# A fused attention and MLP kernel: the row-sum product moves into the MLP's PSUM ring, which goes from two banks to three

## The chip, the cores and the metric

The kernel runs on one core of a Trainium2 chip. The metric is the device time of one execution in microseconds (us); shorter is better. The engines are called as the profile calls them: PE (TensorE, matmul), PEld (its weight loads), DVE (VectorE), ACT (ScalarE), POOL (GpSimd) and SP (which issues transfers).

## The reference, cut to what matters

```python
# attention: 8 batches, 12 heads, 448 positions, head size 64
scores = q @ k.T / 8
e = exp(scores - max)                               # softmax with one more term in the sum
attn = e / (sum(e) + exp(-max) + 1e-9)
x = (attn @ v)  -> 3584 tokens x 768
# MLP: 768 -> 2048 -> 768
h = x @ w_in;  g = relu(h)**2;  out = g @ w_out
```

## The kernel before

The kernel works through 48 pairs of heads ("units"; those of the first batch are cut in two). While a unit's scores, exponentials and values run, TensorE fills its time with matmuls of the MLP of tokens that are already done: generators hand them out in shares (`drain`), between the steps of attention. The MLP's first product works on blocks of 128, 256, 512 or 384 tokens; each of its PSUM tiles ("mp") takes 6 matmuls per 128 features and is then read by a relu and squared.

```python
s_psum  = tile_pool(name="s_psum",  bufs=2, space=PSUM)     # scores: 2 tiles of 2 banks
xz_psum = tile_pool(name="xz_psum", bufs=1, space=PSUM)     # xp and zp: one bank each
m_psum  = tile_pool(name="m_psum",  bufs=2, space=PSUM)     # "mp": 2 banks
...
def row_sums(u, es):                    # sums over the keys, by a product with ones
    zp = xz_psum.tile([128, 512], FP32, name="zp")
    for h in range(2):
        nc.tensor.matmul(zp[64*h:64*h+64, 0:n], ones, of_head(total, u, h), start=True, stop=True)
    nc.scalar.activation(out=lnz, in_=zp, func=AF.Ln, bias=one_b)       # last reader of zp
    nc.scalar.activation(out=rcp, in_=lnz, func=AF.Exp, scale=-1.0)
...
def mlp_in(t0, n):                      # first product of the MLP
    for f0 in range(0, NFFB, per):
        hp = m_psum.tile([128, 512], FP32, name="mp")
        ...                             # matmuls; a yield after each
        if t0 == 0: nc.scalar.activation(out=rt, in_=hp, func=AF.Relu)
        else:       nc.vector.tensor_scalar(out=rt, in0=hp, scalar1=0.0, op0=ALU.max)
        nc.vector.tensor_mul(g, rt, rt)
...
# one unit, in program order
xp = xz_psum.tile([128, 512], FP32, name="xp")
scores(u, et, 0);  drain(share * 0.45);  scores(u, et, 1)
rcp = row_sums(prev, pes);  values(prev, pet, xp, 0);  values(prev, pet, xp, 1)
drain(share * 0.15)
for step in range(3):
    add_chunks(u, et, es, step)         # VectorE sums the exponentials: "es"
    drain(share * (0.15, 0.1, 0.15)[step])
normalise(prev, xp, rcp)                # VectorE: xt = xp * rcp
```

Transposes of the first two batches and idle "warm" matmuls of the start take their tiles from `m_psum` too.

The softmax here doesn't subtract the row's maximum and nothing guards it: scores larger than these inputs give would overflow.

Of the kernel before, what the change touches and what calls it, by code (L numbers as in the profile page):

```python
# [8 lines left out]
FP32 = mybir.dt.float32  # L9
# [6 lines left out]
def kernel(  # L16
# [37 lines left out]
    osb_pool = ctx.enter_context(tc.tile_pool(name="osb", bufs=2))  # L54

    s_psum = ctx.enter_context(tc.tile_pool(name="s_psum", bufs=2, space=bass.MemoryType.PSUM))
    xz_psum = ctx.enter_context(tc.tile_pool(name="xz_psum", bufs=1, space=bass.MemoryType.PSUM))
    m_psum = ctx.enter_context(tc.tile_pool(name="m_psum", bufs=2, space=bass.MemoryType.PSUM))

    ctx.enter_context(tc.manual_schedule())  # L60
    nc.scalar.preload_act_table_set("natural_log_exp_and_others")
# [13 lines left out]
    def load_v(b, p0, p1):  # L75
        hs = slice(2 * p0, 2 * p1)
        if b not in vns:
            vns[b] = v_pool.tile([P, H, RUN, D], FP16, name="vn")
        nc.gpsimd.dma_start(out=vns[b][:, hs], in_=v_r[b, :, hs])  # L79
# [29 lines left out]
    def stage(b):  # L109
        for n, t in (("q", q), ("k", k)):  # L110
            st = nc.dram_tensor(f"stage_{n}{b}", (TOTAL,), FP16, kind="Internal").ap()
            stages[n, b] = st
            src = t.rearrange("b h s d -> (b h s d)")
            lo = b * HSD - FRONT
            hi = min(lo + TOTAL, B * HSD)
            m = (hi - lo) // 1024 * 1024
            for x, y in ((lo, lo + m), (lo + m, hi)):
                if y > x:
                    w = min(y - x, 1024)
                    nc.gpsimd.dma_start(out=st[x - lo:y - lo].rearrange("(r w) -> r w", w=w),  # L120
                                        in_=src[x:y].rearrange("(r w) -> r w", w=w))
            if hi < lo + TOTAL:
                nc.gpsimd.dma_start(out=st[hi - lo:TOTAL].rearrange("(r w) -> r w", r=1),
                                    in_=src[0:lo + TOTAL - hi].rearrange("(r w) -> r w", r=1))
# [11 lines left out]
    def regroup(b, pr):  # L136
        for name in "qk":
            f = flat.tile([P, RUN, 2, D], FP16, name=f"flat{name}")
            nc.vector.tensor_copy(f, naturals[name, b, pr].rearrange("p h t d -> p t h d"))
            flats[name, b, pr] = f  # L140

    def transposes(b, pr):
        tp = m_psum.tile([128, 2, 512], FP16, name="mp")
        for i, name in enumerate("qk"):
            for s in range(RUN):
                nc.tensor.transpose(tp[:, i, P * s:P * s + P], flats[name, b, pr][:, s], ident[0:P, 0:P])  # L146
        if b not in qks:
            qks[b] = qk_pool.tile([128, 3, COLS], FP16, name="qk")
        nc.vector.tensor_copy(qks[b][:, 0:2, pr * S:(pr + 1) * S], tp[:, :, 0:S])
# [13 lines left out]
    def scores(u, et, c):  # L163
        b, pr, q0, n = u
        qk = qks[b]
        two = [] if n == S else s_psum.tile([P, 2, 512], FP32, name="sp")
        for kk in (2 * c, 2 * c + 1):
            sp = s_psum.tile([P, 2, 512], FP32, name="sp") if n == S else two
            if b in ON_PE:
                o = 0 if n == S else kk % 2 * n  # L170
                for h in range(2):
                    r = slice(64 * h, 64 * h + 64)
                    x = pr * S
                    nc.tensor.matmul(sp[:, h, o:o + n], qk[r, 1, x + P * kk:x + P * kk + P],  # L174
                                     qk[r, 0, x + q0:x + q0 + n], start=True, stop=True)
            else:
                for h in range(2):
                    for odd in range(2):
                        r = slice(64 * odd, 64 * odd + 64)
                        x = (2 * pr + h) * (S // 2)  # L180
                        kx = x + kk // 2
                        which = 1
                        if kk % 2 != odd:
                            which = 2
                            kx += kk % 2
                        nc.tensor.matmul(sp[:, odd, h * (S // 2):(h + 1) * (S // 2)],  # L186
                                         qk[r, which, kx:kx + 2 * P - 1:2], qk[r, 0, x:x + S // 2],
                                         start=True, stop=True)
            if n == S:
                exp(chunk(et, u, c, kk).rearrange("p (o x) -> p o x", o=2), sp[:, :, 0:S])  # L190
        if n < S:
            exp(et[:, 0:RUN * 2 * n].rearrange("p (c h x) -> p c h x", c=2, h=2)[:, c], two[:, :, 0:2 * n])
# [16 lines left out]
    def of_head(e, u, h):  # L209

        b, _, _, n = u
        if n < S:
            return e[:, h]
        if b in ON_PE:
            return e.rearrange("p (h x) -> p h x", h=2)[:, h]
        return e.rearrange("p (o h x) -> p h o x", o=2, h=2)[:, h]

    def values(u, et, xp, c):
        b, pr, _, n = u
        for kk in (2 * c, 2 * c + 1):  # L220
            for h in range(2):
                nc.tensor.matmul(xp[64 * h:64 * h + 64, 0:n], vns[b][:, 2 * pr + h, kk, :],  # L222
                                 of_head(chunk(et, u, c, kk), u, h), start=(kk == 0), stop=(kk == RUN - 1))

    def row_sums(u, es):
        n = u[3]
        total = es[:, 0:2 * S] if n == S else es[:, 4 * S - 2 * n:4 * S].rearrange("p (h n) -> p h n", h=2)
        zp = xz_psum.tile([128, 512], FP32, name="zp")
        for h in range(2):
            nc.tensor.matmul(zp[64 * h:64 * h + 64, 0:n], ones, of_head(total, u, h), start=True, stop=True)  # L230
        lnz = z_pool.tile([128, S], FP32, name="lnz")
        rcp = z_pool.tile([128, S], FP32, name="rcp")
        nc.scalar.activation(out=lnz[:, 0:n], in_=zp[:, 0:n], func=AF.Ln, bias=one_b)  # L233
        nc.scalar.activation(out=rcp[:, 0:n], in_=lnz[:, 0:n], func=AF.Exp, scale=-1.0)  # L234
        return rcp

    def normalise(u, xp, rcp):
        b, pr, q0, n = u
        if b // 2 not in xts:
            xts[b // 2] = xt_pool.tile([128, DCH, 2 * S], FP16, name="xt")  # L240
        c = b % 2 * S + q0
        nc.vector.tensor_mul(xts[b // 2][:, pr, c:c + n], xp[:, 0:n], rcp[:, 0:n])  # L242
# [89 lines left out]
    def drain(ns):  # L332
        while work and ns > 0:
            got = next(work[0], None)
            if got is None:
                work.pop(0)
            else:
                ns -= got
                left[0] -= got
# [20 lines left out]
    def keep_warm(n):  # L360
        wp = m_psum.tile([128, 512], FP32, name="mp")
        for _ in range(n):
            nc.tensor.matmul(wp, warm[:, 0:128], warm, start=True, stop=True)  # L363
# [8 lines left out]
    for i in range(NU + 1):  # L372
        u = units[i] if i < NU else None
        prev = units[i - 1] if i > 0 else None
        xp = rcp = None
        if prev:
            pet, pes = et, es
            xp = xz_psum.tile([128, 512], FP32, name="xp")
        if u:
            b, pr = u[0:2]  # L380
            if pr == 0 and 0 < b and b + 1 < B:
                load_v(b + 1, 0, NPAIR)
                stage(b + 1)
            et = e_pool.tile([P, RUN * 2 * S], FP16, name="et")
            es = e_pool.tile([P, 4 * S], FP16, name="es")
            scores(u, et, 0)
            if i == 0:
                keep_warm(8)
            if i in transpose_at:
                transposes(*transpose_at[i])  # L390
            if i in regroup_at:
                regroup(*regroup_at[i])
            if i < NPAIR:
                keep_warm(1)
            drain(share * 0.45)
            scores(u, et, 1)
        if prev:
            rcp = row_sums(prev, pes)
            values(prev, pet, xp, 0)
            values(prev, pet, xp, 1)  # L400
            if i < NPAIR:
                keep_warm(1)
        drain(share * 0.15)
        for step in range(3):
            if u:
                add_chunks(u, et, es, step)
            drain(share * (0.15, 0.1, 0.15)[step])
        if prev:
            normalise(prev, xp, rcp)
            if i - 1 in ready:  # L410
                for part in ready[i - 1]:
                    queue(*part)
                share = left[0] / NPAIR
        if u and b and pr == 2 and b + 1 < B:
            transposed_loads(b + 1)
# [31 lines left out]
```

## Time and profile before

| | before |
|---|---|
| median of 3 runs (range) | 449.58 us (447.37 to 451.88) |
| span of the profiled run, granted clock | 445.8 us, 0.999 |
| PE busy / idle | 426.6 us / 19.2 us |
| DVE busy, ACT busy | 244.7 us, 247.8 us |
| PE waits for the relu (rt) before an mp tile, as listed | 4.8 + 0.5 us |

TensorE is the bound (busy for 426.6 of 445.8 us), so its waits are what counts. Besides the views in the prediction, the chain that ended last shows what stands between the start and the end. This line of it shares the span out by engine:

```profile
PE 74%; DVE 17%; ACT 3%; issue 2%; DMA 2%; POOL 1%; ACTq 0%; POOLq 0%
```

VectorE holds 17% of the chain although TensorE is 96% busy. That share is no estimate of the gain: where TensorE waits for VectorE only briefly, the chain runs through VectorE's work before that wait. Before TensorE's wait of 0.26 us that ends at 156.40, for one, the chain is VectorE's from 150.95 to 156.36.

### The profile page before, as it was taken

What the parts mean: (1) busy time and instruction counts of PE and PEld (TensorE: products, weight loads), DVE (VectorE), ACT (ScalarE), POOL (GpSimd) and SP (SyncE); (2) the same over time, 40 slices, a digit from 0 to 9 for tenths busy, and PEclk for the clock granted to TensorE, in tenths of its full rate; (3) what the DMA queues carried; (4) which work ended last, traced back from release to release, by engine and by line L of the source; (5) the groups of instructions that cost most, each with busy time, mean ns of one, the idle gap of its engine ahead of it and who ended that gap; (6) DMA issues with size and microseconds to landing.
All of it is one profiled execution on the core that took longest, in us unless ns stands there. A gap on an engine that the chain in (4) does not pass through costs nothing.

```text
span 445.8 us, 7533 instructions
## 1 busy us (share of the span) xinstructions
PE 426.6 (96%) x3147; PEld 228.7 (51%) x3147; DVE 244.7 (55%) x487; ACT 247.8 (56%) x361; POOL 33.8 (8%) x52
## 2 busy tenths in 40 slices
PE   8978899999999999999999989999999999999996
PEld 3556554544455545554455544654455545554454
DVE  3767683378722775258832487248662377428700
ACT  2888767754456646674456745764455655650011
POOL 8441100010000100010000100030000000000000
PEclk9999999999999999999999999999999999999999
DMA  9999999199021991279312793039902200010022
GB/s 171 197 197 204 208 202 197 52 191 216 1 64 46 198 179 33 71 124 207 79 37 71 116 217 79 37 62 206 178 1 72 71 1 1 37 37 35 1 71 71
DMA packets 78946, 47.22 MB, mean 106 GB/s; under 512 B 50624, under 2 KB 74944, under 8 KB 78528
## 3 DMA queue, kind: packets, MB, share of 16 engines
q0 software_dynamic: 24608, 22.40, 31.8%
q1 hardware_dynamic: 54304, 24.34, 23.9%
q8 instruction: 24, 0.39, 0.4%
q14 instruction: 10, 0.08, 0.1%
HBM read 45.71 MB, written 19.32 MB: 146 GB/s over the span
## 4 chain that ended last, share of the span: by engine, by line
PE 74%; DVE 17%; ACT 3%; issue 2%; DMA 2%; POOL 1%; ACTq 0%; POOLq 0%
PE mp L279 34%; PE mp L256 20%; PE xp L222 7%; PE sp L186 7%; DVE rt L265 7%; DVE es L199 4%; DVE g L267 3%; PE zp L230 3%; DMA kn<-in_k_dram 2%; ACT et L154 2%; PE sp L174 2%; DVE es L201 1%; DVE xt L242 1%; ACT lnz L233 1%; PE mp L146 1%
## 5 line engine op out<-in xcount | busy, mean ns | idle before, releaser
L154 ACT ACTIVATE et<-sp 112x896 f16<-112x896 f32 (+2 forms) x192 | 166.2, 913 | 125.4 <-PE sp L186 103.9
L256 PE MATMUL mp<-xt,win 128*128 128x512 f16 (+3 forms) x864 | 159.1, 332 | 8.3 <-DVE rt L265 4.8
L279 PE MATMUL mp<-wout,g 128*128 128x512 f16 (+1 forms) x896 | 154.2, 326 | 0.8 <-DVE rt L265 0.5
L256 PEld LDWEIGHTS <-win 128*128 128x128 f16 x864 | 77.3, 98 | 82.8 <-issue 25.7
L279 PEld LDWEIGHTS <-g 128*128 128x128 f16 x896 | 84.2, 98 | 64.6 <-issue 11.5
L199 DVE TENSOR_TENSOR es<-et 112x896 f16<-112x896 f16 x84 | 51.5, 621 | 106.3 <-ACT et L154 106.3
L265 DVE TENSOR_SCALAR rt<-mp 128x512 f16<-128x512 f32 (+1 forms) x120 | 76.0, 633 | 46.2 <-PE mp L256 43.5
L283 ACT ACTIVATE ot<-mp 128x512 f32<-128x512 f32 (+1 forms) x56 | 27.3, 487 | 64.5 <-PE mp L279 63.8
L267 DVE TENSOR_TENSOR g<-rt 128x512 f16<-128x512 f16 (+1 forms) x124 | 49.5, 399 | 7.0 <-ACT rt L263 2.8
L222 PE MATMUL xp<-et,vn 112*64 112x448 f16 (+2 forms) x432 | 45.5, 332 | 0.0
L186 PE MATMUL sp<-qk 64*112 64x224 f16 x576 | 42.8, 268 | 0.0
L186 PEld LDWEIGHTS <-qk 64*112 64x112 f16 x576 | 26.9, 127 | 25.4 <-issue 25.4
L233 ACT ACTIVATE lnz<-zp,one_b 128x448 f32<-128x448 f32 (+2 forms) x54 | 32.2, 596 | 1.9 <-PE zp L230 1.9
L242 DVE TENSOR_TENSOR xt<-xp,rcp 128x448 f16<-128x448 f32 (+2 forms) x54 | 30.5, 565 | 2.7 <-ACT rcp L234 2.7
L234 ACT ACTIVATE rcp<-lnz 128x448 f32<-128x448 f32 (+2 forms) x54 | 28.9, 535 | 1.7
L222 PEld LDWEIGHTS <-vn 112*64 112x64 f16 x432 | 24.0, 110 | 10.2 <-issue 0.2
L79 POOL DMA_DIRECT2D vn<-in_v_dram x10 | 8.9, 889 | 252.4 <-PE xp L222 239.6
L201 DVE TENSOR_TENSOR es<-es 112x896 f16<-112x896 f16 x42 | 26.2, 623 | 1.0
L230 PE MATMUL zp<-es,ones 112*64 112x448 f16 (+2 forms) x108 | 19.4, 356 | 1.0 <-DVE es L207 0.9
L174 PE MATMUL sp<-qk 64*112 64x192 f16 (+2 forms) x144 | 16.8, 308 | 1.6 <-ACT et L154 1.3
L363 PE MATMUL mp<-warm 128*128 128x512 f16 x31 | 10.7, 444 | 1.2 <-DVE warm L301 1.2
L174 PEld LDWEIGHTS <-qk 64*112 64x112 f16 x144 | 6.8, 124 | 9.4 <-issue 6.5
(32 smaller groups left out, 80.3 us busy)
## 6 DMA issues: line engine op xcount, KB each, us to landing
out_dram<-ot SPq DMA_DIRECT2D x12, 384.0 KB, 2.4
vn<-in_v_dram POOLq DMA_DIRECT2D x6, 672.0 KB, 8.8
stage_q<-in_q_dram POOLq DMA_DIRECT2D x5, 676.0 KB, 10.9
stage_k<-in_k_dram POOLq DMA_DIRECT2D x5, 676.0 KB, 13.7
win<-in_moe_w_in_dram POOLq DMA_DIRECT2D x8, 384.0 KB, 14.6
wout<-in_moe_w_out_dram POOLq DMA_DIRECT2D x4, 768.0 KB, 20.4
out_dram<-ot SPq DMA_DIRECT2D x8, 288.0 KB, 2.6
out_dram<-ot SPq DMA_DIRECT2D x8, 192.0 KB, 2.7
```

The costliest lines, as they stand in the source:

```text
L154: nc.scalar.activation(out=out_, in_=in_, func=AF.Exp, scale=scale)
L174: nc.tensor.matmul(sp[:, h, o:o + n], qk[r, 1, x + P * kk:x + P * kk + P], qk[r, 0, x + q0:x + q0 + n], start=True, stop=True)
L186: nc.tensor.matmul(sp[:, odd, h * (S // 2):(h + 1) * (S // 2)], qk[r, which, kx:kx + 2 * P - 1:2], qk[r, 0, x:x + S // 2], start=True, sto ...
L199: nc.vector.tensor_add(f[:, step], e[:, 2 * step], e[:, 2 * step + 1])
L222: nc.tensor.matmul(xp[64 * h:64 * h + 64, 0:n], vns[b][:, 2 * pr + h, kk, :], of_head(chunk(et, u, c, kk), u, h), start=(kk == 0), stop=(k ...
L230: nc.tensor.matmul(zp[64 * h:64 * h + 64, 0:n], ones, of_head(total, u, h), start=True, stop=True)
L233: nc.scalar.activation(out=lnz[:, 0:n], in_=zp[:, 0:n], func=AF.Ln, bias=one_b)
L242: nc.vector.tensor_mul(xts[b // 2][:, pr, c:c + n], xp[:, 0:n], rcp[:, 0:n])
L256: nc.tensor.matmul(hp[:, j * n:(j + 1) * n], win[:, dc, fb * 128:(fb + 1) * 128], xt[:, dc, x0:x0 + n], start=(dc == 0), stop=(dc == DCH - 1))
L265: nc.vector.tensor_scalar(out=rt[:, 0:m], in0=hp[:, 0:m], scalar1=0.0, scalar2=None, op0=ALU.max)
L267: nc.vector.tensor_mul(g[:, 0:m], rt[:, 0:m], rt[:, 0:m])
L279: nc.tensor.matmul(op[:, 0:n1 - n0], gt[fb][:, ts * 128:(ts + 1) * 128], wout[:, fb, n0:n1], start=(fb == 0), stop=(fb == NFFB - 1))
```

## The change

Its intent: zp uses a bank of its own for a short part of each unit. If it takes its tile from the ring of the MLP instead, its bank can be the MLP's third. Counted by their tiles, the pools have 8 banks in both kernels: 4 for the scores, 1 + 1 for xp and zp and 2 for mp before; 4, 1 and 3 after.

```diff
-    xz_psum = ctx.enter_context(tc.tile_pool(name="xz_psum", bufs=1, space=bass.MemoryType.PSUM))
-    m_psum = ctx.enter_context(tc.tile_pool(name="m_psum", bufs=2, space=bass.MemoryType.PSUM))
+    x_psum = ctx.enter_context(tc.tile_pool(name="x_psum", bufs=1, space=bass.MemoryType.PSUM))
+    m_psum = ctx.enter_context(tc.tile_pool(name="m_psum", bufs=3, space=bass.MemoryType.PSUM))
...
-        zp = xz_psum.tile([128, 512], FP32, name="zp")
+        zp = m_psum.tile([128, 512], FP32, name="mp")
...
-            xp = xz_psum.tile([128, 512], FP32, name="xp")
+            xp = x_psum.tile([128, 512], FP32, name="xp")
```

No instruction is added, removed or moved on any engine. In the profile of the changed kernel zp is called mp; it is known by its line, L230.

## The prediction

> **What bounds the kernel now.** I read the page first, then the waits of TensorE, then the timeline of one stretch with many waits, and last the start of every matmul, one by one.
>
> The page says that TensorE sets the time:
>
> ```profile
> PE 426.6 (96%) x3147; PEld 228.7 (51%) x3147; DVE 244.7 (55%) x487; ACT 247.8 (56%) x361; POOL 33.8 (8%) x52
> ```
>
> Only 445.8 − 426.6 = 19.2 us of the span shows TensorE idle. The view of who waited for whom, for TensorE, says for what (total us, times, longest):
>
> ```profile
> PE mp L256 <- DVE rt L265: 4.8, 13, 0.6
> PE mp L256 <- DVE xt L242: 1.7, 2, 1.5
> ...
> PE mp L146 <- ACT rt L263: 0.9, 2, 0.7
> ...
> PE mp L256 <- DVE qk L149: 0.6, 1, 0.6
> PE mp L279 <- DVE rt L265: 0.5, 1, 0.5
> ```
>
> All but the second line are waits for a bank of the MLP's ring: a new "mp" tile can't start until VectorE's relu (rt, L265), or another reader, has left the bank. The second is a wait for data and stays. By this view the change has 6.8 us to gain, 1.5%. But matmuls overlap: one of 384 columns is shown 326 ns long, while the next starts 162 ns after it. A wait of w at a tile's start costs w + 164 ns, and one under 164 ns shows no idle at all. So I took, for each first matmul of an mp tile, the distance from the start before it, less the steady distance (216, 162, 109 ns for 512, 384, 256 columns). That gives the real loss by stage of the MLP's first product (t0 is the token block):
>
> - blocks of 512 tokens, three of them beside attention (89 to 118 us, and 104 us and 208 us later): 0.28 + 0.30 + 0.49 = 1.07 us each
> - blocks of 384, three (146 to 171 us, same steps): 0.26 + 0.45 + 0.42 + 0.79 + 0.21 + 0.26 = 2.39 us each
> - the block of 256 (48 to 65 us): 0.49 + 0.65 = 1.14 us
> - the start (28 to 41 us): 0.81 + 0.74 + 0.28 = 1.83 us
> - the last block, with no attention beside it (400 to 421 us), and all second products: none.
>
> Together 3.2 + 7.2 + 1.1 + 1.8 = 13.3 us, 3%: that is the ceiling. The timeline of a 384 stage shows how it arises (start, length, engine, last what ended the idle time before):
>
> ```profile
> 154.41 0.55 DVE L265 TENSOR_SCALAR rt<-mp 128x384 f16<-128x384 f32 x1
> 154.99 0.36 DVE L267 TENSOR_TENSOR g<-rt 128x384 f16<-128x384 f16 x1
> 155.01 1.14 PE L256 MATMUL mp<-xt,win 128*128 128x384 f16 x6 [0.29 <-DVE rt L265]
> 155.26 0.62 DVE L242 TENSOR_TENSOR xt<-xp,rcp 128x448 f16<-128x448 f32 x1
> 155.80 0.55 DVE L265 TENSOR_SCALAR rt<-mp 128x384 f16<-128x384 f32 x1
> 156.22 3.63 SPq L129 DMA_TRANSPOSE qk<-stage_q  x1
> 156.38 0.36 DVE L267 TENSOR_TENSOR g<-rt 128x384 f16<-128x384 f16 x1
> 156.40 1.30 PE L256 MATMUL mp<-xt,win 128*128 128x384 f16 x7 [0.26 <-DVE rt L265]
> 156.66 0.55 DVE L265 TENSOR_SCALAR rt<-mp 128x384 f16<-128x384 f32 x1
> ...
> 159.68 0.64 ACT L233 ACTIVATE lnz<-zp,one_b 128x448 f32<-128x448 f32 x1
> ...
> 160.24 0.56 DVE L265 TENSOR_SCALAR rt<-mp 128x384 f16<-128x384 f32 x1 [1.72 <-PE mp L256]
> ```
>
> VectorE interleaves the relus with the sums and the normalising of attention (es, xt, 0.62 us each), so it falls a tile behind and TensorE waits; then TensorE leaves the MLP for scores, zp and values, and VectorE sits idle for 1.72 us. The two starve each other by turns. That is what a deeper ring mends: VectorE isn't short of time, only of a buffer.
>
> [...] the same six losses come back in all three 384 stages within 4 ns. [...]
>
> **The change part by part.** It adds and removes no instruction: in the built programs PE has 6296 rows in both, in the same order, and the other engines do too. Only banks change. In the built program a new tile takes the bank that was given back first, zp included, so I read the bank of each tile off both programs. A bank is now reused two mp tiles and a zp, or three mp tiles, later.
>
> *A 384 stage.* Call its 16 tiles T1 to T16, z1 to z3 the zp tiles that fall inside T3, T9 and T14, R the first tile of the second product. T6 to T8 started at 152.96, 155.01, 156.40; T9 157.37, z2 158.15, T12 162.78, T14 165.57, R 170.45. A tile takes 6 × 0.162 = 0.97 us. Banks before: T6 after T4, T7 after T5, T8 after T6, T12 after T10, T14 after T12, R after T15. Now: T6 after T3, T7 after T4, T8 after T5, T9 after T6, z2 after T7, T12 after T9, T14 after T11, R after T14.
> - T6: T3's relu ended 151.51. Starts 152.70, 0.26 ahead.
> - T7: T4's relu ended 152.90. 155.01 − 0.26 − 0.45 = 154.30.
> - T8: 155.27; T5's relu ended 154.96. No wait.
> - T9: could start 156.24; T6's relu ends 155.80 + 0.55 = 156.35 (VectorE is busy without a break from 150.95 to 158.53, so it can't be earlier), and 0.05 to hand over: 156.40. Ahead 0.97, with 0.16 waited.
> - z2: 157.18; T7's relu ends 157.21, so 157.26. Ahead 0.89.
> - T12: T9's relu, as much earlier, is long done. 0.79 more: ahead 1.68.
> - T14: 0.21 more, R: 0.26 more. Ahead 2.15 of 2.39.
>
> *A 512 stage.* The same walk finds every bank free in time: the closest, the tile at 101.56, waits for a relu that ended 99.91 and wants it at 100.98. All 1.07 us.
>
> *The 256 block.* 0.49 + 0.65, both from a tile whose relu is done: 1.14 us.
>
> *The start.* The chain there is mixed. At 30.47 TensorE waits 0.81 for a transposed bank; freed, the next exponentials start 0.6 earlier, when ScalarE is done with a relu. At 36.61 the gain (0.74) mostly dies, as the following zp waits for the sums, which wait for ScalarE. At 40.38 0.28. I take 1.0 of 1.83.
>
> Sum: 3 × 2.15 + 3 × 1.07 + 1.14 + 1.0 = 11.8 us. As TensorE is the bound in all of these but the start, all of it comes off the end. I take off half a us for hand-overs I can't place: 11.3 us, 449.6 − 11.3 = 438.3.
>
> **The rivals.**
> 1. VectorE is the bound in the 384 stages, and a third bank only gives one tile of credit (0.97 us) per stage. For it: the unbroken 7.6 us. Against it: three idle stretches of 1.7 us in the stage (before 150.95, 160.24, 168.44). It would make 11.3 − 3 × 1.2 = 7.7, so 441.9.
> 2. zp, now in the ring, brings ScalarE's lateness in. Its bank is given back when the logarithm (lnz) ends: 159.68 + 0.64 − 158.15 = 2.2 us after zp starts, as two exponentials stand before it. Then mp tiles wait for lnz. Against it: the tile after zp in the bank comes later: T5 starts 0.37 after z1's lnz ends. But T16's margin is 0.04 (169.21 to 169.17). Were it 0.2 late in each of the 18 units beside the first product: 3.6 us lost, 442. In the second product tiles last 16 × 0.216 = 3.5 us and 1.8 us, so it can't bite.
> 3. zp itself waits for a relu, and holds back the values, xp and the next scores: in the walk only z2, by 0.08.
> 4. Something else ends each stage (exponentials, the transposing loads), and the gain dries up. Against it: second products run at 100% PE, the exponentials wait for PE by 2.2 us.
>
> **Range and chances.** The walk is worked for one stage of each kind, and the stages repeat. 2% is 9.0 us, 2.3 under my sum; rivals 1 and 2 each land just short of it. The runs of before spread by ±0.5%. Range 435.5 to 442.0; faster by over 2%: 0.82, same 0.17, slower 0.01.
>
> **What would show it.** The wait "mp L256 <- DVE rt" should fall from 4.8 us to under 0.6, "mp L279 <- DVE rt" to nothing, "L146 <- ACT rt" to nothing. A wait of zp for rt, about 3 × 0.1 us, should appear. Waits of mp for lnz would prove rival 2; waits of 0.3 us or more for rt left in 384 stages rival 1. 384 stages (T1 to R) should last 22.2 us in place of 24.3, 512 stages 27.1 in place of 28.1. TensorE's busy time should fall too, though nothing is removed, since a shown duration hides 164 ns of each wait. I'd be wrong if new waits of zp or scores take up over 3 us.

## The result, and the profile after

The changed kernel took 436.62 us (median of 4 runs, 436.03 to 437.17), the kernel before 449.34 in the same rounds. The ratio is 0.9714, with a 95% interval of 0.9662 to 0.9765: faster by over 2%. A ratio is the mean time of one kernel's fast runs over that of the other's of the same rounds, so it isn't quite the ratio of the medians. Two later repeats gave 0.9737 each (0.9705 to 0.9768 and 0.9705 to 0.9769).

The head of the profile after, and its chain:

```profile
PE 423.7 (97%) x3147; PEld 230.4 (53%) x3147; DVE 244.4 (56%) x487; ACT 248.2 (57%) x361; POOL 33.2 (8%) x52
...
PE 91%; ACT 3%; DMA 2%; issue 1%; DVE 1%; POOL 1%; ACTq 0%; POOLq 0%
```

The counts and VectorE's and ScalarE's work are what they were. VectorE has left the chain (17% to 1%). TensorE's busy time fell by 2.9 us although it does the same matmuls, since part of each wait used to hide inside the shown length of a matmul (up to 164 ns of it at 384 columns: 326 shown, less the 162 from start to start). (In the repeat below, whose clock was whole, it fell by 4.3 us, to 422.3.)

All that TensorE still waits for (us in total, times, longest):

```profile
PE mp L256 <- DVE xt L242: 1.7, 2, 1.5
PE mp L230 <- DVE es L207: 1.6, 3, 0.9
PE mp L146 <- DVE flatk L139: 1.4, 3, 0.6
PE sp L174 <- ACT et L154: 1.3, 4, 0.4
PE mp L363 <- DVE warm L301: 1.2, 1, 1.2
PE sp L174 <- DVE qk L149: 0.2, 1, 0.2
```

No mp tile waits for a relu any more, in either product, and none waits for the logarithm (lnz) that reads zp. Every wait left lies in the first 50 us. One has grown: zp waits for the sums (es L207) 1.6 us in place of 0.9.

The timeline of the 384 stage that the prediction walks through, after (VectorE's, ScalarE's and TensorE's rows of T6 to T11):

```profile
152.13 2.76 PE L256 MATMUL mp<-xt,win 128*128 128x384 f16 x15
...
153.97 0.55 DVE L265 TENSOR_SCALAR rt<-mp 128x384 f16<-128x384 f32 x1
...
155.43 0.38 PE L230 MATMUL mp<-es,ones 112*64 112x448 f16 x2
...
156.50 3.26 PE L256 MATMUL mp<-xt,win 128*128 128x384 f16 x19
156.87 0.64 ACT L233 ACTIVATE lnz<-mp,one_b 128x448 f32<-128x448 f32 x1
157.52 0.56 DVE L265 TENSOR_SCALAR rt<-mp 128x384 f16<-128x384 f32 x1 [0.89 <-PE mp L256]
```

Before, TensorE stopped twice between T6 and T9, and VectorE then stood idle for 1.72 us. Now the 15 matmuls show no idle time between them (0.15 us is still lost at T9, too short for the view), and VectorE's idle time is 0.89 us: TensorE comes back to the MLP earlier, as it waits less. Between its returns after one zp and the next pass 8.09 us (148.41 to 156.50), and before the change 8.97 (150.25 to 159.22).

Where the time came from, by the starts of the matmuls (which are the same, in the same order, in both kernels). "Second profile" is the repeat `after_again`, in which the clock was 1.00 throughout:

| stretch | before | first profile after | second profile after |
|---|---|---|---|
| start, from the transposes near 29 us to those near 48 us | 18.74 us | 18.43 | 17.88 |
| block of 256 | 16.61 | 15.47 | 15.48 |
| block of 512, each of three | 28.14 | 27.08 | 27.08 |
| block of 384, each of three | 24.33 | 22.20 | 22.20 |
| from the end of the last 384 block to the last matmul | 62.84 | 62.84 | 62.84 |

The gains of the second profile are 0.86 + 1.13 + 3 × 1.06 + 3 × 2.13 = 11.6 us; 0.34 us more came before 29 us. It is not counted as the change's: neither trace lists a wait for an MLP bank there, and the three profiles of the changed kernel themselves differ by 0.22 us at the first matmul of the MLP (24.36 to 24.58 us; 24.69 before). The spans say the same: 445.8 − 433.8 = 12.0 us.

### The profile page after: what moved, and what is told of

It reads as the page before.

```text
span 435.4 us, 7530 instructions
## 1 busy us (share of the span) xinstructions
PE 423.7 (97%) x3147; PEld 230.4 (53%) x3147; DVE 244.4 (56%) x487; ACT 248.2 (57%) x361; POOL 33.2 (8%) x52
## 4 chain that ended last, share of the span: by engine, by line
PE 91%; ACT 3%; DMA 2%; issue 1%; DVE 1%; POOL 1%; ACTq 0%; POOLq 0%
PE mp L279 34%; PE mp L256 34%; PE sp L186 9%; PE xp L222 8%; PE mp L230 3%; DMA kn<-in_k_dram 2%; PE sp L174 2%; ACT et L154 2%; ACT lnz L233 1%; PE mp L146 1%; DVE es L203 0%; ACT rcp L234 0%; POOL qn L91 0%; DVE xt L242 0%; POOL vn L79 0%
## 5 line engine op out<-in xcount | busy, mean ns | idle before, releaser
L256 PE MATMUL mp<-xt,win 128*128 128x512 f16 (+3 forms) x864 | 156.4, 334 | 1.7 <-DVE xt L242 1.7
L256 PEld LDWEIGHTS <-win 128*128 128x128 f16 x864 | 78.2, 99 | 71.9 <-issue 12.7
L233 ACT ACTIVATE lnz<-mp,one_b 128x448 f32<-128x448 f32 (+2 forms) x54 | 32.2, 596 | 2.0 <-PE mp L230 1.9
L242 DVE TENSOR_TENSOR xt<-xp,rcp 128x448 f16<-128x448 f32 (+2 forms) x54 | 30.5, 566 | 2.7 <-ACT rcp L234 2.7
L230 PE MATMUL mp<-es,ones 112*64 112x448 f16 (+2 forms) x108 | 19.4, 355 | 1.8 <-DVE es L207 1.6
L230 PEld LDWEIGHTS <-ones 112*64 112x64 f16 x108 | 6.4, 106 | 11.2 <-issue 5.7
```

The lines of the kernel that those rows point to most:

```text
L230: nc.tensor.matmul(zp[64 * h:64 * h + 64, 0:n], ones, of_head(total, u, h), start=True, stop=True)
L233: nc.scalar.activation(out=lnz[:, 0:n], in_=zp[:, 0:n], func=AF.Ln, bias=one_b)
L242: nc.vector.tensor_mul(xts[b // 2][:, pr, c:c + n], xp[:, 0:n], rcp[:, 0:n])
L256: nc.tensor.matmul(hp[:, j * n:(j + 1) * n], win[:, dc, fb * 128:(fb + 1) * 128], xt[:, dc, x0:x0 + n], start=(dc == 0), stop=(dc == DCH - 1))
```

## The experiments

The theory: with two banks, VectorE, which is interrupted by attention's sums, is late for a moment and TensorE has no bank to go on in; a third bank bridges that. Rivals: VectorE is the real bound in the 384 stages; two banks are too few whatever VectorE does; it is moving zp that helps, not the bank; part of the gain is something else. Ten runs followed, two of them the changed kernel again.

### after_again: the changed kernel once more

No edit. The first profiles gave 10.4 us of span where the medians gave 12.7, so this asks which is right.

> The changed kernel once more, unchanged, against the kernel before. The two profiles so far differ by 10.4 us of span, the medians by 12.7. Theory (a third bank ends the alternate waiting of TensorE and VectorE): the walk gives 10.8 us outside the start plus what the start gives, so a gain of 10.5 to 12 us (ratio 0.973 to 0.977) when the runs share rounds and the clock is whole; with the granted clock at 1.00 in the start of the profiled run, the zp tile near 31 us starts 0.2 to 0.7 us ahead of before, not 0.6 us behind as in the first profile. Rival (part of the gain is something the walk does not know): the gain stays at 12.5 us or more, or the start stays behind at a whole clock.

Measured: 436.84 us (435.6 to 438.81, 6 runs), ratio 0.9737. The profiled run had a clock of 1.00 and a span of 433.8 us, and the zp tile near 31 us (30.1) was 0.95 us ahead of before. The theory's numbers hold; 0.95 lies over its 0.2 to 0.7, as 0.34 came from the first 29 us.

What set the first profile behind is shown by the same stretch of the two profiles (window; then busy time and instructions of PE, PEld, DVE, ACT and POOL; granted clock; DMA share; GB/s). First profile of the changed kernel:

```profile
24.00:27.70 3.70, 2.23 (x34) 1.39 (x28) 1.59 (x4) 3.06 (x6) 1.53 (x2) 1.00 1.45 197
27.70:31.00 3.30, 3.30 (x33) 2.67 (x30) 2.05 (x5) 2.36 (x4) 1.48 (x2) 0.53 1.45 199
```

Second profile:

```profile
27.70:31.00 3.30, 3.18 (x49) 2.45 (x48) 2.72 (x7) 3.27 (x6) 1.22 (x2) 1.00 1.44 198
```

In the first, TensorE ran at about half its clock (0.53) for 3.3 us, right after a stretch in which it stood idle for 1.47 us of 3.7 (waiting for xt). It did 33 matmuls in the time of 49. The second profile has the same 2.23 us of work from 24.0 to 27.7 us, and no such spell after it. The runs of this kernel come at mean clocks of 1.00, 0.996 and 0.992, with spans of 433.8 to 434.7, 435.4 and 436.8 to 437.0 us: steps of some 1.5 us, about what 3.3 us at half clock cost (half of it, 1.65). In the trace the spell is 3.41 us at a clock of 0.50, from 27.87 us; half of that is 0.004 of a span of 435 us, one step. The profile of `after_third`, with a mean clock of 0.992, has two, from 27.1 and from 47.6 us. The kernel before probably has such spells too: its runs have clocks from 0.988 to 1.00, though its one profile has none in the start. Compared at equal clock, in the last rounds, the kernels differ by spans of about 12.0 us at 1.00 (446.4 to 434.35), 11.6 at 0.996 (447.2 to 435.55) and 11.4 at 0.992 (448.35 to 437.0), each the mean of two or three runs. So the gain is about 11.6 us, and the 12.7 of the first medians probably had most of one such spell's luck in it.

### before_nosums: two banks, VectorE without its sums

```diff
@@ add_chunks @@
         if n == S:
+            return
@@ row_sums @@
-        total = es[:, 0:2 * S] if n == S else ...
+        total = pet_of[0][:, 0:2 * S] if n == S else ...      # the exponentials of the first chunk
```

> The kernel before, two mp banks, but without VectorE's three sums (es) in the units of 448 columns; zp then sums only a part, so the result is wrong on purpose. Theory (TensorE waited because VectorE, interrupted by attention's work, was late for a moment, with too few banks to bridge it): with the sums gone VectorE is not late, the wait of L256 for rt falls from 4.8 us to under 1 us, and the time falls by 8 to 11 us with no bank added, to 438 to 441. Rival (two banks are too few whatever VectorE does, for instance as the hand-over of a bank itself takes too long): time and waits stay within 3 us of before.

Measured: 437.43 us (435.44 to 439.64, 4 runs), ratio 0.9744; the result is wrong, as meant. Nothing was added, and the time is that of the changed kernel. TensorE's waits (lines are 3 further down in this file: L259 is the first product's matmul):

```profile
PE mp L259 <- DVE xt L245: 1.5, 1, 1.5
...
PE mp L146 <- ACT rt L266: 0.9, 2, 0.7
...
PE mp L259 <- DVE qk L149: 0.4, 1, 0.4
```

The fall of 11.3 us is a little more than the 8 to 11 expected. The waits of the first product for VectorE's relu are gone; those of the start, whose sums were left in, are not. The stages: 512 blocks 27.08 us, 384 blocks 21.97, start 18.52. So two banks are enough once VectorE is spared the sums, and the rival falls.

### after_nosums: three banks, VectorE without its sums

The same edit on the changed kernel.

> The changed kernel, three banks, without the same sums (wrong result on purpose). Theory: the third bank already took away what the sums caused, so removing them as well gives at most the 0.7 us that the walk left (0.15 at T9 and 0.08 at z2 in each 384 stage): within 1.5 us of the changed kernel, 435 to 437. Rival (VectorE is still the bound in the 384 stages with three banks): 3 us or more faster than the changed kernel.

Measured: 436.83 us (435.36 to 437.9), ratio 0.9727; 384 blocks 21.97 us, 512 blocks 27.08. Without the sums the third bank is worth 0.6 us of the medians, with them 11.9; taking the sums away is worth 11.3 us with two banks, and nothing that the medians show with three. The two remedies remove the same loss. Freeing VectorE of 64 us of work (busy 244.4 to 180.0 us) shortens a 384 block by 0.23 us only, which is what the walk had left at T9 and z2. VectorE is not the bound there.

### share_two: zp in the ring, but no third bank

```diff
-    m_psum = ctx.enter_context(tc.tile_pool(name="m_psum", bufs=3, space=bass.MemoryType.PSUM))
+    m_psum = ctx.enter_context(tc.tile_pool(name="m_psum", bufs=2, space=bass.MemoryType.PSUM))
```

> Half of the change: zp takes its tile from the MLP's ring, but the ring keeps two banks, and the bank set free lies idle. Theory (the gain is the bank; zp in the ring costs a hold until the logarithm has read it): the mp tile after each zp takes zp's bank, so it must wait until lnz ends: 0.3 to 1.0 us in the units beside the first product. Slower than before by 4 to 14 us, about 457, with a new wait of L256 for ACT lnz of some 5 us. Rival (moving zp off its own bank helps or costs nothing, e.g. by where the banks lie): within 2 us of before, or faster.

Measured: 462.38 us (460.39 to 462.6), ratio 1.0285 (1.0244 to 1.0326): slower by 2.9%. Part of that is clock (its profiled run has a mean clock of 0.988: by estimate, 0.012 of 460.7 us taken twice, some 11 us at half clock): at a mean clock of 0.996 its one run had a span of 458.6 us and those of before 446.4 to 447.0 in the same rounds, some 12 us. The first of TensorE's waits:

```profile
PE mp L256 <- ACT lnz L233: 9.0, 15, 0.9
PE mp L256 <- DVE rt L265: 2.8, 9, 0.3
PE mp L279 <- ACT lnz L233: 1.9, 5, 0.9
```

zp in the ring is not free: it holds its bank until ScalarE's logarithm has read it, and with two banks the next mp tile needs just that one. In one unit of this trace zp starts at 157.71 us, the logarithm ends at 159.88, and TensorE, idle for 0.49 us, goes on at 159.93. The wait was sized at some 5 us and is 9.0, and the second product has it as well, which the expectation had not. So the bank is what helps, by more than the sharing costs.

### ring_four: xp in the ring too, four banks

```diff
-    x_psum = ctx.enter_context(tc.tile_pool(name="x_psum", bufs=1, space=bass.MemoryType.PSUM))
-    m_psum = ctx.enter_context(tc.tile_pool(name="m_psum", bufs=3, space=bass.MemoryType.PSUM))
+    m_psum = ctx.enter_context(tc.tile_pool(name="m_psum", bufs=4, space=bass.MemoryType.PSUM))
...
-            xp = x_psum.tile([128, 512], FP32, name="xp")        # at the head of the unit
...
             rcp = row_sums(prev, pes)
+            xp = m_psum.tile([128, 512], FP32, name="mp")
```

> The change taken one step further: xp too takes its tile from the MLP's ring, only just before its first matmul, and the ring gets all four banks. Theory (after the third bank only 0.16 us at T9 and 0.08 us at z2 are left in each 384 stage, 0.72 us in all, and every other tile finds its bank free): 384 stages 21.97 us in place of 22.20, 512 stages 27.08 as they are, the whole 0.7 to 0.9 us shorter than the changed kernel at the same clock (span 432.9 to 433.2 at a clock of 1.00, against 433.8), which is within the noise of the medians. Rival (a deeper ring goes on paying as the third bank did): 3 us or more. Second rival (xp holds its bank until the normalising multiply and now delays mp tiles): 384 or 512 stages longer than in the changed kernel, a wait of L256 for xt L242 in them.

Measured: 437.43 us (435.51 to 437.7, 5 runs), ratio 0.9744. The 384 blocks took 22.01 us, the 512 blocks 27.08, with no wait for xt in them. That is the theory's small gain, 0.19 us a block (0.23 expected), far below what the medians can show. The span expected at a clock of 1.00 was not tested, as no run had it; the best, at 0.998, took 433.7 us. A fourth bank has almost nothing left to bridge.

### after_relu_dve: the first block's relu on VectorE

```diff
-            if t0 == 0:
-                nc.scalar.activation(out=rt[:, 0:m], in_=hp[:, 0:m], func=AF.Relu)
-            else:
-                nc.vector.tensor_scalar(...)
+            nc.vector.tensor_scalar(...)
```

> The changed kernel with the relu of the first token block (128 tokens) on VectorE in place of ScalarE. The start gave 0.86 us where its three losses were 1.83, as the zp tile near 38 us still waits 0.9 us for the sums (es), which stand on VectorE behind a relu that ScalarE gives late. Theory: with that relu on VectorE the wait of zp for es L207 falls from 1.6 us to about 0.7, and the start (from the transposes at 28.6 us to those at 46.5 us) takes 17.1 to 17.5 us in place of 17.88; the rest is as it was, so 0.4 to 0.8 us off the span at the same clock. Rival (the start hangs on ScalarE's exponentials or on the loads whatever stands before zp): start within 0.2 us of 17.88, or longer.

Measured: 436.59 us (436.47 to 438.0, 4 runs), ratio 0.975. The start took 17.50 us with the last 0.9 us of a half-clock spell in it. The changed kernel's profiles took 17.88 with none, 18.11 (`after_third`, 0.5 us of one spell and 0.6 of another) and 18.43 (1.6 us of one). The wait of zp for es L207 fell to 1.1 us, not to 0.7. So in this profile the start hangs in part on the chain relu on ScalarE, square, sums, zp; the profile of four_relu_warm, below, does not bear it out. The whole is not told from the changed kernel by its median; all four runs had clocks of 0.994 or 0.995.

### warm_start: idle matmuls in TensorE's idle time near 26 us

```diff
+            if i == NPAIR + 1:
+                keep_warm(6)
             drain(share * 0.45)
```

> The changed kernel with six idle matmuls (warm, 512 columns, 1.3 us) put on TensorE before the first product's first tile, where TensorE idles 1.47 us for xt near 26 us. In the first profile of the changed kernel the granted clock is 0.53 from 27.7 to 31.0 us, just after that idle time, and 1.00 in the second profile; the runs of every kernel come at clocks of about 1.00, 0.996 or 0.992, and spans some 1.6 us apart. Theory (the difference of 10.4 us in the first profiles to 11.9 in the second is one such spell at half clock after the idle time, chance in when it falls, and nothing of the banks): with the idle time filled the spell after it goes, most runs come at 0.998 or above, and the median span is 433.8 to 434.5, 1 to 2 us under the changed kernel's. Rival (the spells come whatever TensorE does there): the clocks spread as before, medians equal within 0.7 us, or slower by the added work.

Measured: 436.40 us (436.01 to 437.29, 6 runs), ratio 0.9717, median span 434.6. Five of six runs had a clock of 0.999 or more, one 0.996; of 16 runs of the changed kernel, seven had 1.00 and four 0.992. The theory's clocks came, its median was missed by 0.1 us of span, and against the changed kernel (436.62 to 437.31) the medians part by less than the spread of runs. That the idle time brings the spell is likely by these counts, and not shown; the same idle time without a spell in the second profile, and the spell from 47.6 us in `after_third`, say that it isn't the whole story.

### four_relu and four_relu_warm: the small edits together

The edits of ring_four and after_relu_dve; then those and warm_start's. To compare the latter fairly the changed kernel ran a third time in the same rounds (after_third). Expected of four_relu:

> The two edits that the traces of single experiments showed to take something off, together: xp in a ring of four with late allocation (384 stages 22.01 in place of 22.20 us) and the first block's relu on VectorE (start some 0.7 us shorter at the same clock). Theory: they add up, 3 x 0.19 + 0.7 = 1.3 us off the changed kernel at the same clock: a span of 432.4 to 433.0 at a clock of 1.00, or 434.0 to 434.6 at 0.996; ratio to before about 0.971. Rival (they get in each other's way in the start, where VectorE's relus hold the ring): start longer than 17.5 us at a whole clock, and the span within 0.5 us of the changed kernel's.

Of four_relu_warm:

> All three small edits together: the ring of four with xp in it, the first block's relu on VectorE, and six idle matmuls in the idle time near 26 us. Theory: the 1.3 us of the first two stay, and the third keeps the granted clock at 0.998 or above in most runs, so a median span of 432.5 to 433.5 and a median time of 434.3 to 435.3, 1.5 to 2.5 us under the changed kernel in the same rounds (ratio to it 0.9945 to 0.9965). Rival (the medians of the single edits did not part from the changed kernel's, and the sum won't either): within 0.8 us of the changed kernel.

Of after_third:

> The changed kernel a third time, so that the version of three small edits is compared on the same chip in the same rounds. Both theories: ratio to before 0.972 to 0.976, median 436.2 to 437.2, clocks between 0.992 and 1.00 with spans about 1.5 us apart for each 0.004 of clock; 384 stages 22.20, 512 stages 27.08 us in the profile.

Measured: four_relu 436.16 us (435.44 to 437.26, 6 runs), ratio 0.9711. Its one run at a clock of 1.00 had a span of 433.9 us, a miss of 0.9; its two at 0.996 had 434.4, as expected. The rival's test, the start at a whole clock, wasn't possible in it: the profiled run had a clock of 0.50 from 26.4 to 33.2 us.

four_relu_warm took 435.51 us (435.11 to 436.1, 5 runs), ratio 0.9694 (0.9662 to 0.9727), after_third 437.31 us (436.03 to 439.32, 6 runs; 0.1 over the range expected), ratio 0.9737 (0.9705 to 0.9769). All five runs of the former had clocks of 0.998 or more; the latter's went down to 0.992. At a clock of 1.00 the spans are 433.3 and 433.4 against 434.3 and 434.4: 1.0 us, where the theory had 1.3. The rest of the 1.8 us between the medians is clock. The profile of four_relu_warm makes the rival's test after all: at a whole clock its start took 18.46 us, longer than the rival's 17.5 and than the changed kernel's 17.88. TensorE waited 0.5 us there for flatk, the copy of a loaded k, at 39.2, and on VectorE the sums, now behind a relu, then held up zp by 0.8 us at 41.2. Its 384 blocks kept their 0.19 us each (22.01). So that the relu's move shortens the start is not shown. The intervals overlap, so this version beats the kernel before clearly, and the changed kernel by some 0.4% that these runs make likely and don't settle.

## Why the prediction was right

The time, 436.62 us, lies in the range (435.5 to 442.0), and "faster" came. Point by point:

- **TensorE's waits as the ceiling, counted from starts.** Right. The waits view alone had 6.8 us to give; the measured gain of about 11.6 us could only be seen by starts, since a wait costs the shown idle time and 164 ns more (326 less 162, at 384 columns). The three waits that were to fall (mp for rt in both products, the transposes for rt) fell to nothing.
- **The 384 stage, 2.15 us of 2.39.** Measured 24.33 − 22.20 = 2.13. The two waits that the walk left are there: T9 started 314 ns after the matmul before it, 152 over the steady 162 (walk: 0.16 us), and z2 84 ns late (walk: 0.08). The waits view doesn't list them, as both are shorter than the overlap of matmuls; the prediction's "a wait of zp for rt should appear" was wrong of that view, by its own rule.
- **The 512 stage, 1.07, and the 256 block, 1.14.** Measured 1.06 (28.14 − 27.08) and 1.14 (16.61 − 15.47).
- **The start, 1.0 of 1.83.** Measured 0.86 in the profile at full clock. The gap near 30.5 us gave 0.61 (predicted 0.6); the one near 36.6 gave 0.74 and lost all of it at the following zp, as foretold; the one near 40.4 gave 0.25 (0.28).
- **Half a us off for hand-overs.** Not needed; nothing of that kind was lost. That and, in all likelihood, the luck of the clock in the first medians put the centre 1.7 us too high; 0.24 us of it is the kernel before, whose median was 449.34 in these rounds and 449.58 in the prediction.
- **Rival 1, VectorE as the bound:** shown wrong by after_nosums (0.23 us a block). **Rival 2, zp's late logarithm:** with three banks no mp tile waits for lnz, although T16's margin was 0.04 us before; zp and the logarithm moved forward with TensorE. With two banks the same hold costs 2.9% (share_two), so the mechanism is real, and the third bank is what keeps it harmless. **Rival 3:** only z2, as said. **Rival 4:** the stages keep all of their gain; outside the start nothing is given back.

What the prediction didn't have is the half-clock spell in the start, which moves single runs by 1.5 us, more than most terms of its sum.

## What to carry to other kernels

When a bound engine and its helper starve each other by turns, as here, suspect a missing buffer before a slow helper: see whether the helper is idle elsewhere in the same stretch (VectorE was, for 1.72 us), then walk one period with the new buffer order, tile by tile. The two-by-two of banks and sums told the two apart here: 448.8 us with neither remedy, 437.4 with fewer sums, 436.8 with the bank, 436.8 with both. Count a pipelined engine's waits from start to start, not by its idle time: 13.3 us of losses were listed as 6.8 us of waits. A short-lived tile with a bank of its own is a place to find that buffer, but here moving it into the ring paid only with the bank that it brought along: without it the time rose by 2.9%.
